# A decode block on one core: `wo` in four loads instead of eight, `w2` in one, the last K ahead of three V, three of the twelve q copies moved to ScalarE, one end barrier less

## The chip, the cores and the metric

One Trainium2 chip, one core used. The metric is the device time of one execution in microseconds (us), median of several runs. The profiler's *span*, from the first to the last recorded instruction of the core, is given for every run too; the rest of the time lies outside it.

## The reference, cut to what matters

```python
B, D, Hq, Dh, W, F = 4, 640, 32, 192, 2048, 1536        # bf16 inputs, one token per batch row
xn = layernorm(x)
q  = xn @ wq                                            # 640 x 6144
p  = softmax(q . k_cache[:, :, -W:, :] * Dh ** -0.5)    # per batch row and head
o  = p . v_cache[:, :, -W:, :]
out = x + o @ wo + (silu(xn @ w1) * (xn @ w3)) @ w2     # wo 6144 x 640, w1 and w3 640 x 1536
```

K and V windows are 32 heads of 3 MB each; with the weights, 223 MB have to come in for very little arithmetic.

## The kernel before

Every head has one K and one V transfer of 3 MB, issued by one queue in program order, K into a ring of two buffers, V into one of three. VectorE (DVE) multiplies K by q, TensorE (PE) adds up the products, a chain over four engines makes the softmax weights `z`, PE multiplies them with V. The projections by `wo` and the feed-forward part run between the heads. Cuts are marked `...`.

The start: `xn`, then q. A K buffer is free for the third head only after the products of the first head, and these need q.

```python
xn = const.tile([B, D], BF16, name="xn")
nc.vector.tensor_scalar_mul(out=xn[:], in0=xc[:], scalar1=rstd[:, 0:1])     # DVE
...
for i, qp in enumerate(qps):                       # 2 x 6 pieces of q, out of PSUM
    dst = qbc[:, (c0 + i) * QC:(c0 + i + 1) * QC]
    if i % 2:
        nc.vector.tensor_copy(out=dst, in_=qp[:])
    else:
        nc.scalar.copy(out=dst, in_=qp[:])
```

The weights `w1`. Its 640 rows do not divide evenly; 64 odd rows lie on a few partitions whose other rows have to be zero, and GpSimd clears them:

```python
we = wopool.tile([LF, 2 * F], BF16, tag="wo", name="w1e")     # LF = 44
nc.gpsimd.memset(we[:], 0.0)                                  # 44 x 3072
nc.gpsimd.memset(wt[0:LF, FH:], 0.0)                          # 44 x 1536
```

The end: the last loads, in this order, and what PE does behind them.

```python
for h in range(H - 2, H):
    add(NU - 6, 0, load_v, h)                # ... K31 is issued between V29 and V30
add(NU - 6, 0, w2_load, 0)                   # w2: columns 0-4, 4-8, 8-11, 11-12 of 12
add(NU - 6, 0, w2_load, 1)
add(NU - 6, 0, wo_load, NG - 2)              # wo: groups of 4 heads, NG = 8
add(NU - 6, 0, wo_load, NG - 1)
add(NU - 6, 0, w2_load, 2)
add(NU - 6, 0, w2_load, 3)
...
nc.scalar.dma_start(out=out..., in_=res[...])
```

## Time and profile before

| | kernel before |
|---|---|
| time, median of 3 runs | 525.95 us (525.63 to 526.19) |
| span of the profiled run | 523.8 us |
| last landing of data | 520.75 us |
| DVE makes `xn` | 11.35 to 13.39 us |
| first product K times q | 32.25 us |
| third K issued | 41.62 us |

How to read it: the transfers fill the whole span (the load queue's packets take 99.2% of the 16 engines' time), so an engine matters only where it delays the *issue* of a transfer or works on after the last landing (at the end). The prediction below shows the profile lines for this and reads them.

### The profile page before, as it was taken

The numbers are of one execution on the slowest core, as the hardware profiler recorded it, in microseconds if no ns is written. First come the engines' busy times: TensorE is split into PE (matmuls) and PEld (weight loads), VectorE is DVE, ScalarE is ACT, GpSimd is POOL, SyncE is SP. The second block draws the span as 40 slices with busy tenths as digits, with TensorE's granted clock in tenths as the row PEclk, the third lists the DMA queues.
The fourth block names the chain that finished last, engine by engine and source line by source line (L and its number), as shares of the span: only waits on it lengthen the run. The fifth ranks groups of instructions, "written<-read, shape, count | busy, mean of one in ns | idle before, by whom it ended". The sixth has DMA issues, their size and how long they took to land.

```text
span 523.8 us, 4820 instructions
## 1 busy us (share of the span) xinstructions
PE 361.8 (69%) x2336; PEld 75.9 (14%) x1643; DVE 340.9 (65%) x413; ACT 55.8 (11%) x176; POOL 5.6 (1%) x12
## 2 busy tenths in 40 slices
PE   0965866887668776667547768586686876675685
PEld 0100111121111111111111111111111111111122
DVE  3268853687656767577646877466667766667671
ACT  2111111111001110101100111001101110011111
POOL 4000000000000000000000000000000000000000
PEclk9979886898878998789997988889878898889988
DMA  9999999999999999999999999999999999999996
GB/s 389 422 443 425 433 431 432 428 433 432 430 435 428 437 418 446 424 437 426 434 434 429 432 434 429 435 427 435 425 437 434 427 437 431 430 434 425 441 418 275
DMA packets 11904, 223.26 MB, mean 426 GB/s; under 512 B 1332, under 2 KB 1608, under 8 KB 3052
## 3 DMA queue, kind: packets, MB, share of 16 engines
q1 hardware_dynamic: 11868, 222.96, 99.2%
q8 instruction: 15, 0.25, 0.2%
q14 instruction: 5, 0.04, 0.0%
q10 hardware_dynamic: 16, 0.01, 0.0%
HBM read 222.96 MB, written 0.01 MB: 426 GB/s over the span
## 4 chain that ended last, share of the span: by engine, by line
DMA 60%; PE 20%; DVE 15%; ACT 3%; issue 1%; SPq 1%
DMA kt<-in_A_k_cache_dram 44%; PE ps L288 11%; DMA w<-in_B_w_dram 11%; DVE pr L277 10%; DMA vt<-in_A_v_cache_dram 5%; PE po L361 4%; PE qps L243 3%; DVE sc L296 2%; ACT ex L324 1%; DVE z L332 1%; DMA x_sb<-in_A_x_dram 1%; PE mt L318 1%; ACT L324 0%; ACT negm L321 0%; PE mt L305 0%
## 5 line engine op out<-in xcount | busy, mean ns | idle before, releaser
L288 PE MATMUL ps<-pr,idb 128*128 128x512 bf16 x768 | 214.7, 422 | 137.6 <-DVE pr L277 137.5
L277 DVE TENSOR_TENSOR pr<-kt,qbc 128x3072 bf16<-128x3072 bf16 x128 | 223.5, 1746 | 104.0 <-DMA kt<-in_A_k_cache_dram 104.0
L296 DVE TENSOR_REDUCE sc<-ps 128x16 f32<-128x512 f32 x128 | 87.1, 681 | 2.7 <-PE ps L288 2.6
L340 PE MATMUL o_ps<-vt,z 128*8 128x384 bf16 x1024 | 60.5, 380 | 0.2 <-DVE z L332 0.2
L361 PE MATMUL po<-o_sb,sel_w 128*32 128x192 f32 x128 | 49.2, 518 | 0.6 <-ACT o_sb L343 0.6
L340 PEld LDWEIGHTS <-z 128*8 128x8 bf16 x1024 | 26.2, 95 | 98.8 <-issue 89.2
L332 DVE TENSOR_TENSOR z<-ex,mask_b 128x256 bf16<-128x256 bf16 x32 | 13.5, 423 | 38.6 <-ACT ex L324 38.6
L343 ACT COPY o_sb<-o_ps 128x384 f32<-128x384 f32 x32 | 15.3, 478 | 196.9 <-PE o_ps L340 196.9
L313 ACT ACTIVATE gneg<-gmax 1x128 f32<-1x128 f32 x32 | 9.8, 308 | 162.8 <-DVE gmax L310 162.8
L305 PEld LDWEIGHTS mt<-idf,lmax 128*1 128x1 f32 x32 | 3.2, 101 | 127.5 <-issue 125.5
L361 PEld LDWEIGHTS po<-o_sb,sel_w 128*32 128x32 f32 x128 | 13.8, 130 | 29.4 <-issue 27.9
L288 PEld LDWEIGHTS <-idb 128*128 128x128 bf16 x124 | 12.0, 97 | 39.3 <-issue 32.8
L318 PEld LDWEIGHTS mt<-ones_ff,gneg 1*128 1x128 f32 x64 | 9.6, 186 | 47.1 <-issue 43.7
L243 PE MATMUL qps<-wt,xnT 128*128 128x512 bf16 x59 | 14.9, 412 | 0.1
L318 PE MATMUL mt<-ones_ff,gneg 1*128 1x1 f32 x64 | 12.3, 259 | 0.7 <-ACT gneg L313 0.7
L321 ACT COPY negm<-mt 128x1 f32<-128x1 f32 x32 | 5.1, 159 | 70.4 <-PE mt L318 70.4
L310 DVE TENSOR_REDUCE gmax<-mt 1x4 f32<-1x128 f32 x32 | 8.8, 274 | 5.8 <-PE mt L305 5.8
L348 PEld LDWEIGHTS po<-rsum,tot_w 128*32 128x32 f32 x64 | 4.4, 108 | 51.5 <-ACT ex L324 35.4
L249 DVE CAST qbc<-qps 128x512 bf16<-128x512 f32 x6 | 3.8, 684 | 11.7 <-PE qps L243 11.7
L324 ACT ACTIVATE ex<-sc,negm 128x64 bf16<-128x64 f32 x32 | 11.1, 348 | 1.0
L305 PE MATMUL mt<-idf,lmax 128*1 128x128 f32 x32 | 10.9, 340 | 0.0
L199 PE MATMUL xnT_ps<-idb,xn 4*128 4x4 bf16 x5 | 0.4, 178 | 13.4 <-DVE xn L194 13.4
(74 smaller groups left out, 84.4 us busy)
## 6 DMA issues: line engine op xcount, KB each, us to landing
kt<-in_A_k_cache_dram SPq DMA_DIRECT2D x32, 3072.0 KB, 19.1
vt<-in_A_v_cache_dram SPq DMA_DIRECT2D x32, 3072.0 KB, 25.5
wo_t<-in_A_wo_dram SPq DMA_DIRECT2D x8, 960.0 KB, 20.7
wt<-in_A_wq_dram SPq DMA_DIRECT2D x2, 3072.0 KB
w<-in_B_w_dram SPq DMA_DIRECT2D x1, 1920.0 KB
wt<-in_A_wq_dram SPq DMA_DIRECT2D x1, 1536.0 KB, 19.5
w<-in_B_w_dram SPq DMA_DIRECT2D x1, 1536.0 KB
w<-in_B_w_dram SPq DMA_DIRECT2D x2, 640.0 KB
```

Source lines behind the costliest of these rows:

```text
L243: nc.tensor.matmul(qp[:], lhsT=xnT[:, kc].rearrange("p a b -> p (a b)"), rhs=wq_rows[kc][:, (c0 + i) * QC:(c0 + i + 1) * QC], start=(kc == ...
L277: nc.vector.tensor_tensor(out=pr[:], in0=kts[h][:, g * JQ:(g + 1) * JQ, :], in1=qbc[:, h * Dh:(h + 1) * Dh].unsqueeze(1).to_broadcast([P, ...
L288: nc.tensor.matmul(ps[:], lhsT=idb[:], rhs=pr[:, :, kk * DD:(kk + 1) * DD], start=(kk == 0), stop=(kk == NK - 1))
L296: nc.vector.tensor_reduce(out=scs[h][:, g * JQ:(g + 1) * JQ], in_=pss.pop(u)[:], axis=AX.X, op=ALU.add)
L305: nc.tensor.transpose(out=mt[0:1, 0:P], in_=chs[h][0][:], identity=idf[:])
L313: nc.scalar.activation(out=gneg[:], in_=gmax[:].unsqueeze(1).to_broadcast([1, PB, B]), func=ACTF.Copy, scale=-SCALE)
L318: nc.tensor.matmul(mt[:, P:P + 1], lhsT=gneg[:].rearrange("o p b -> o (p b)"), rhs=ones_ff[:], start=True, stop=True)
L324: nc.scalar.activation(out=ex[:], in_=scs.pop(h)[:], func=ACTF.Exp, bias=negm[:, 0:1], scale=SCALE, accum_out=rsum[:])
L332: nc.vector.tensor_tensor(out=z[:], in0=ex[:].unsqueeze(2).to_broadcast([P, NJ, B]), in1=mask_b[:].unsqueeze(1).to_broadcast([P, NJ, B]), ...
L340: nc.tensor.matmul(o_ps[c * CT:c * CT + 2 * B, :], lhsT=z[:, 2 * jj:2 * jj + 2, :], rhs=vt[:, 2 * jj:2 * jj + 2, :], start=(jj < 4), stop= ...
L343: nc.scalar.copy(out=o_sb[:], in_=o_ps[:])
L361: nc.tensor.matmul(po[sl, 0:Dh], lhsT=sel_w[:, par].rearrange("p a b -> p (a b)"), rhs=o_sb[:, par * Dh:(par + 1) * Dh].rearrange("p (r i) ...
```

## The change

Its intent: fewer and larger packets (`wo` by eight heads, so four loads of 1.9 MB, the last one in three pieces; `w2` in one; the odd `w1` rows in two transfers instead of four), softmax weights of the last head ready before its V, DVE free of the second half of the q copies (three of its six move to ScalarE), and no second barrier behind the clear of the semaphores. With one `wo` buffer instead of two, the odd rows' tile can be larger, and takes all of them. The diff, cut to its core:

```diff
+def one_end_barrier(nc):
+    ...                      # drops all behind the last clear but one GpSimd drain
-    HG: int = 4,
+    HG: int = 8,
+    FG: int = 4,
-    wopool = ctx.enter_context(tc.tile_pool(name="wo", bufs=2))
+    wopool = ctx.enter_context(tc.tile_pool(name="wo", bufs=1))
 def load_k(h):
-        kt = kpool.tile([P, NJ, Dh], BF16, tag="kt")
+        kt = (kpool if h < H - 1 else vpool).tile(...)      # K31 in the V ring, V31 in the K ring
-            if i % 2:
+            if i % 2 and c0 == 0:
                 nc.vector.tensor_copy(out=dst, in_=qp[:])
 def w1_load():
-        we = wopool.tile([LF, 2 * F], BF16, tag="wo", name="w1e")
+        we = wopool.tile([LF, LS, F], BF16, tag="wo", name="w1e")     # LS = 5
         nc.gpsimd.memset(we[:], 0.0)
-        nc.gpsimd.memset(wt[0:LF, FH:], 0.0)
+    early = {H - 1: (NU - 10, -1)}                          # K31 ahead of V29, V30, V31
-    add(NU - 6, 0, w2_load, 0)                              # and 1, wo, wo, w2 2, w2 3
+    WOC = [0, RPP - 5, RPP - 2, RPP]
+    add(NU - 6, 0, w2_load)
+    for i0, i1 in zip(WOC, WOC[1:]):
+        add(NU - 6, 0, wo_load, NG - 1, i0, i1)
```

More of the change, by code (lines that the diff above doesn't have):

```diff
@@ L47, in first_load_first @@
         head.instructions.insert(j, ins)
+def one_end_barrier(nc):
+    for f in nc.python_module().functions:
+        end = f.blocks[2]
+        i = next(i for i, ins in enumerate(end.instructions) if isinstance(ins, mybir.InstISA))
+        keep = next(j for j in range(i + 1, len(end.instructions)) if end.instructions[j].engine == mybir.EngineType.Pool)
+        assert isinstance(end.instructions[keep], mybir.InstDrain)
+        for j in range(len(end.instructions) - 1, i, -1):
+            ins = end.instructions[j]
+            assert isinstance(ins, (mybir.InstDrain, mybir.InstEventSemaphore)), ins
+            if j != keep:
+                del end.instructions[j]
 @with_exitstack
@@ L87 @@
     CT = 32
+    HB = HG * CT // P
     QW = HG * Dh
     RPP = QW // P
+    RW = Dh // RPP
     NU = H * GQ
@@ L95 @@
     assert JQ * DD == 512 and JQ % 2 == 0 and 2 * Dh <= 512 and 2 * N0 == D and N0 <= 512
-    assert (H * Dh) % QC == 0 and NQ % 6 == 0 and QW % P == 0 and Dh == CT * RPP and P == HG * CT and F == HG * CT * FC
-    assert 2 * H * Dh <= NJ * Dh and KBUFS == 2 and VBUFS == 3
+    assert (H * Dh) % QC == 0 and NQ % 6 == 0 and QW % P == 0 and Dh == RW * RPP and CT == HB * RW and P == FG * CT and F == FG * CT * FC
+    assert 2 * H * Dh <= NJ * Dh and KBUFS == 2 and VBUFS == 3 and HB * (Dh + 1) <= 512 and H // HG > 1
     nc.at_finalize(keep_loaded_weights)
     nc.at_finalize(first_load_first)
+    nc.at_finalize(one_end_barrier)
     ctx.enter_context(tc.manual_schedule())
@@ L123, in load_k @@
     def load_k(h):
-        kt = kpool.tile([P, NJ, Dh], BF16, tag="kt")
+        kt = (kpool if h < H - 1 else vpool).tile([P, NJ, Dh], BF16, tag="kt" if h < H - 1 else "vt", name="kt")
         nc.sync.dma_start(out=kt[:].rearrange("q j d -> q (j d)"),
@@ L127, in load_k, with load_v, wo_load @@
         kts[h] = kt
-    def load_v(h, n=1):
-        vt = vpool.tile([P, NJ, Dh], BF16, tag="vt")
-        for j in range(0, NJ, NJ // n):
-            nc.sync.dma_start(out=vt[:, j:j + NJ // n].rearrange("q j d -> q (j d)"),
-                              in_=v_win[:, h].rearrange("b (p j) d -> p b j d", p=PB)[:, :, j:j + NJ // n].rearrange("p b j d -> p b (j d)"))
-        vts[h] = vt
-    def wo_load(hg):
-        wo_t = wopool.tile([P, RPP * D], BF16, tag="wo")
-        nc.sync.dma_start(out=wo_t[:], in_=A_wo[hg * QW:(hg + 1) * QW, :].rearrange("(p i) n -> p (i n)", i=RPP))
-        wos[hg] = wo_t
+    def load_v(h):
+        vt = (vpool if h < H - 1 else kpool).tile([P, NJ, Dh], BF16, tag="vt" if h < H - 1 else "kt", name="vt")
+        nc.sync.dma_start(out=vt[:].rearrange("q j d -> q (j d)"),
+                          in_=v_win[:, h].rearrange("b (p j) d -> p b (j d)", p=PB))
+        vts[h] = vt
+    def wo_load(hg, i0=0, i1=RPP):
+        if i0 == 0:
+            wos[hg] = wopool.tile([P, RPP * D], BF16, tag="wo", name="wo_t")
+        nc.sync.dma_start(out=wos[hg][:, i0 * D:i1 * D],
+                          in_=A_wo[hg * QW:(hg + 1) * QW, :].rearrange("(p i) n -> p i n", i=RPP)[:, i0:i1, :].rearrange("p i n -> p (i n)"))
     x_sb = const.tile([B, D], BF16, name="x_sb")
@@ L201 @@
     nc.vector.tensor_copy(out=xnT[:], in_=xnT_ps[:].unsqueeze(2).to_broadcast([P, KC, PB, B]))
-    KM, PH, LE, LI = KC - 1, P // 2, 3, 4
-    LP, LF, LB = LE * LI, CT + LE * LI, KM * P + PH
-    assert D - LB == 5 * LP + LI and F % LE == 0
+    KM, LE, LI, LS = KC - 1, 3, 4, 5
+    LP, LF = LE * LI, CT + LE * LI
+    PH = D - KM * P - LP * LS - LI
+    LB = KM * P + PH
+    assert PH == P // 2 and F % LE == 0
     xm = ppool.tile([B, 2, PH, 2], BF16, tag="pr", name="xm")
@@ L212 @@
         nc.vector.tensor_copy(out=xm[:, i, :, i], in_=xn[:, KM * P:LB])
-    xe = ppool.tile([B, 3 + LE, LF], BF16, tag="pr", name="xe")
+    xe = ppool.tile([B, LS + LE, LF], BF16, tag="pr", name="xe")
     nc.gpsimd.memset(xe[:], 0.0)
-    for g in range(2):
-        b0 = LB + g * 2 * LP
-        nc.vector.tensor_copy(out=xe[:, 0:2, g * CT:g * CT + LP].rearrange("b s (e i) -> b s e i", i=LI),
-                              in_=xn[:, b0:b0 + 2 * LP].rearrange("b (i e s) -> b s e i", e=LE, s=2))
-    nc.vector.tensor_copy(out=xe[:, 2, 0:LP].rearrange("b (e i) -> b e i", i=LI),
-                          in_=xn[:, LB + 4 * LP:LB + 5 * LP].rearrange("b (i e) -> b e i", e=LE))
+    nc.vector.tensor_copy(out=xe[:, 0:LS, CT:LF].rearrange("b s (e i) -> b s e i", i=LI),
+                          in_=xn[:, LB:LB + LS * LP].rearrange("b (i e s) -> b s e i", e=LE, s=LS))
     for e in range(LE):
-        nc.vector.tensor_copy(out=xe[:, 3 + e, CT + e * LI:CT + (e + 1) * LI], in_=xn[:, LB + 5 * LP:D])
-    NX = KM + 2
-    xw_ps = ps_t.tile([P, NX + 3 + LE, B], BF16, tag="t", name="xw_ps")
+        nc.vector.tensor_copy(out=xe[:, LS + e, e * LI:(e + 1) * LI], in_=xn[:, LB + LS * LP:D])
+    xw_ps = ps_t.tile([P, KM + 2 + LS + LE, B], BF16, tag="t", name="xw_ps")
     for kc in range(KM):
@@ L228, with weights @@
         nc.tensor.transpose(out=xw_ps[:, KM + i, :], in_=xm[:, i].rearrange("b r h -> b (r h)"), identity=idb[0:B, 0:B])
-    for i in range(3 + LE):
-        nc.tensor.transpose(out=xw_ps[0:LF, NX + i, :], in_=xe[:, i, :], identity=idb[0:B, 0:B])
-    xw = const.tile([P, NX, NREP, B], BF16, name="xw")
-    nc.vector.tensor_copy(out=xw[:], in_=xw_ps[:, 0:NX, :].unsqueeze(2).to_broadcast([P, NX, NREP, B]))
-    xl = const.tile([LF, 3 + LE, NREP, B], BF16, name="xl")
-    nc.vector.tensor_copy(out=xl[:], in_=xw_ps[0:LF, NX:, :].unsqueeze(2).to_broadcast([LF, 3 + LE, NREP, B]))
+    for i in range(LS + LE):
+        nc.tensor.transpose(out=xw_ps[0:LF, KM + 2 + i, :], in_=xe[:, i, :], identity=idb[0:B, 0:B])
+    def weights(name, p, c0, c1):
+        t = const.tile([p, c1 - c0, NREP, B], BF16, name=name)
+        nc.vector.tensor_copy(out=t[:], in_=xw_ps[0:p, c0:c1, :].unsqueeze(2).to_broadcast([p, c1 - c0, NREP, B]))
+        return t
+    xw = weights("xw", P, 0, KM)
+    xh = weights("xh", P, KM, KM + 2)
+    xl = weights("xl", LF, KM + 2, KM + 2 + LS + LE)
     qbc = const.tile([P, H * Dh], BF16, name="qbc")
@@ L268, in acc_add @@
             acc_half(i, lhsT, rhs, last=last)
-    po = ps_po.tile([P, Dh + 1], FP32, name="po")
+    po = ps_po.tile([P, HB * (Dh + 1)], FP32, name="po")
+    po_v = po[:, 0:HB * Dh].rearrange("p (i x r) -> p i x r", x=HB, r=RW)
     def x_add(i):
@@ L346, in ge_tot @@
     def ge_tot(h):
-        sl = slice((h % HG) * CT, (h % HG + 1) * CT)
-        nc.tensor.matmul(po[sl, Dh:Dh + 1], lhsT=tot_w[:].rearrange("p a b -> p (a b)"), rhs=rsums.pop(h)[:],
-                         start=True, stop=True)
+        blk, x = (h % HG) // HB, h % HB
+        nc.tensor.matmul(po[blk * CT:(blk + 1) * CT, HB * Dh + x:HB * Dh + x + 1], lhsT=tot_w[:].rearrange("p a b -> p (a b)"),
+                         rhs=rsums.pop(h)[:], start=True, stop=True)
         chs.pop(h)
     def ge_rec(hg):
-        rt = small.tile([P, 1], FP32, tag="rt", bufs=2, name="rt")
@@ L354, in ge_rec @@
-        nc.vector.reciprocal(out=rt[:], in_=po[:, Dh:Dh + 1])
+        rt = small.tile([P, HB], FP32, tag="rt", bufs=2, name="rt")
+        nc.vector.reciprocal(out=rt[:], in_=po[:, HB * Dh:HB * (Dh + 1)])
         rts[hg] = rt
     def ge_sum(h):
-        sl = slice((h % HG) * CT, (h % HG + 1) * CT)
+        blk, x = (h % HG) // HB, h % HB
         o_sb = o_sbs.pop(h)
         for par in range(2):
-            nc.tensor.matmul(po[sl, 0:Dh], lhsT=sel_w[:, par].rearrange("p a b -> p (a b)"),
+            nc.tensor.matmul(po_v[blk * CT:(blk + 1) * CT, :, x, :], lhsT=sel_w[:, par].rearrange("p a b -> p (a b)"),
@@ L362, in ge_sum @@
                              rhs=o_sb[:, par * Dh:(par + 1) * Dh].rearrange("p (r i) -> p i r", i=RPP), start=(par == 0), stop=(par == 1))
     def ge_turn(hg):
-        og = small.tile([P, RPP, CT], BF16, tag="og", bufs=1, name="og")
-        nc.vector.tensor_scalar_mul(out=og[:].rearrange("p i r -> p (i r)"), in0=po[:, 0:Dh],
-                                    scalar1=rts.pop(hg)[:, 0:1])
+        og = small.tile([P, RPP, HB, RW], BF16, tag="og", bufs=1, name="og")
+        nc.vector.tensor_tensor(out=og[:], in0=po_v, in1=rts.pop(hg)[:].unsqueeze(1).unsqueeze(3).to_broadcast([P, RPP, HB, RW]),
+                                op=ALU.mult)
@@ L368, in ge_turn, with ge_proj @@
         oT = small.tile([P, RPP, CT], BF16, tag="oT", bufs=2, name="oT")
-        nc.vector.transpose(out=oT[:].rearrange("p i r -> p (i r)"), in_=og[:].rearrange("p i r -> p (i r)"))
+        nc.vector.transpose(out=oT[:].rearrange("p i r -> p (i r)"), in_=og[:].rearrange("p i x r -> p (i x r)"))
         oTs[hg] = oT
-    def ge_proj(hg, i0, i1):
+    def ge_proj(hg, i0, i1, last=False):
         oT, wo_t = oTs[hg], wos[hg]
         for i in range(i0, i1):
-            acc_add(oT[:, i, 0:B], wo_t[:, i * D:(i + 1) * D])
@@ L378 @@
-    FW = F // HG
+            acc_add(oT[:, i, 0:B], wo_t[:, i * D:(i + 1) * D], last=last and i == RPP - 1)
+    FW = F // FG
     sT = const.tile([P, FW], FP32, name="sT")
@@ L382 @@
     ffn = {}
-    FM, FH = KM * F, KM * F + F // 2
+    FM = KM * F
     def w1_load():
-        w = B_w1
-        wt = fpool.tile([P, FH + F], BF16, tag="w", name="w1")
-        we = wopool.tile([LF, 2 * F], BF16, tag="wo", name="w1e")
+        wt = fpool.tile([P, FM + F // 2], BF16, tag="w", name="w1")
+        we = wopool.tile([LF, LS, F], BF16, tag="wo", name="w1e")
         nc.gpsimd.memset(we[:], 0.0)
-        nc.gpsimd.memset(wt[0:LF, FH:], 0.0)
-        nc.sync.dma_start(out=wt[:, 0:FM], in_=w[0:KM * P, :].rearrange("(p kc) n -> p (kc n)", kc=KM))
-        nc.sync.dma_start(out=wt[:, FM:FH], in_=w[KM * P:LB, :].rearrange("r (h n) -> (r h) n", h=2))
+        nc.sync.dma_start(out=wt[:, 0:FM], in_=B_w1[0:KM * P, :].rearrange("(p kc) n -> p (kc n)", kc=KM))
+        nc.sync.dma_start(out=wt[:, FM:], in_=B_w1[KM * P:LB, :].rearrange("r (h n) -> (r h) n", h=2))
         ffn["w1"], ffn["w1e"] = wt, we
     def w1_low(n):
-        w, wt, we = B_w1, ffn["w1"], ffn["w1e"]
-        if n < 2:
-            b0 = LB + n * 2 * LP
-            nc.sync.dma_start(out=we[n * CT:n * CT + LP, :],
-                              in_=w[b0:b0 + 2 * LP, :].rearrange("(i e s) n -> e i (s n)", e=LE, s=2))
-        elif n == 2:
-            nc.sync.dma_start(out=wt[0:LP, FH:FH + F], in_=w[LB + 4 * LP:LB + 5 * LP, :].rearrange("(i e) n -> e i n", e=LE))
+        b0, we = LB + LS * LP, ffn["w1e"]
+        if n == 0:
+            nc.sync.dma_start(out=we[CT:LF].rearrange("p s n -> p (s n)"),
+                              in_=B_w1[LB:b0, :].rearrange("(i e s) n -> e i (s n)", e=LE, s=LS))
         else:
-            nc.sync.dma_start(out=wt[CT:LF, FH:FH + F // LE], in_=w[LB + 5 * LP:D, :].rearrange("i (e n) -> e i n", e=LE))
+            nc.sync.dma_start(out=we[0:LP, 0, 0:F // LE], in_=B_w1[b0:D, :].rearrange("i (e n) -> e i n", e=LE))
     def w1_in():
@@ L411, in mm @@
         def mm(w, lhsT, rhs, c0=0, start=False, stop=False):
-            nc.tensor.matmul(ps[w * CT:(w + 1) * CT, c0:c0 + rhs.shape[1]], lhsT=lhsT.rearrange("p a b -> p (a b)"), rhs=rhs,
-                             start=start, stop=stop)
+            nc.tensor.matmul(ps[w * CT:(w + 1) * CT, c0:c0 + rhs.shape[1]], lhsT=lhsT.rearrange("p a b -> p (a b)"), rhs=rhs, start=start, stop=stop)
         def main(kc):
-            for w in range(HG):
+            for w in range(FG):
                 mm(w, xw[:, kc], wt[:, kc * F + w * FW:kc * F + (w + 1) * FW], start=(kc == 0), stop=(kc == KM - 1))
         main(0)
-        for w in range(HG):
+        for w in range(FG):
             c0 = FM + (w % 2) * FW
-            mm(w, xw[:, KM + w // 2], wt[:, c0:c0 + FW])
-        for i in range(2):
-            for w in range(HG):
-                mm(w, xl[:, i], we[:, i * F + w * FW:i * F + (w + 1) * FW])
-        for w in range(HG):
-            mm(w, xl[:, 2], wt[0:LF, FH + w * FW:FH + (w + 1) * FW])
+            mm(w, xh[:, w // 2], wt[:, c0:c0 + FW])
+        for i in range(LS):
+            for w in range(FG):
+                mm(w, xl[:, i], we[:, i, w * FW:(w + 1) * FW])
         FE = F // LE
         for e in range(LE):
-            for w in range(HG):
+            for w in range(FG):
                 c0, c1 = max(e * FE, w * FW), min((e + 1) * FE, (w + 1) * FW)
                 if c0 < c1:
-                    mm(w, xl[:, 3 + e], wt[0:LF, FH + c0 - e * FE:FH + c1 - e * FE], c0 - w * FW)
+                    mm(w, xl[:, LS + e], we[:, 0, c0 - e * FE:c1 - e * FE], c0 - w * FW)
         for kc in range(1, KM):
@@ L444, in w3_in @@
         for kc in range(KC):
-            for w in range(HG):
+            for w in range(FG):
                 nc.tensor.matmul(ffn["ps"][w * CT:(w + 1) * CT, :], lhsT=xnT[:, kc].rearrange("p a b -> p (a b)")[:, 0:CT],
@@ L458, with w2_load, ffn_out @@
     w2_v = B_w2.rearrange("(p c) n -> p c n", c=FC)
-    W2C = [0, FC - 8, FC - 4, FC - 1, FC]
-    def w2_load(i):
-        if i == 0:
-            ffn["w2"] = fpool.tile([P, FC, D], BF16, tag="w", name="w2")
-        c0, c1 = W2C[i:i + 2]
-        nc.sync.dma_start(out=ffn["w2"][:, c0:c1, :].rearrange("p c n -> p (c n)"),
-                          in_=w2_v[:, c0:c1, :].rearrange("p c n -> p (c n)"))
-    def ffn_out(i):
-        for c in range(*W2C[i:i + 2]):
-            acc_add(hT[:, c, 0:B], ffn["w2"][:, c, :], last=(c == FC - 1))
+    def w2_load():
+        wt = fpool.tile([P, FC, D], BF16, tag="w", name="w2")
+        nc.sync.dma_start(out=wt[:].rearrange("p c n -> p (c n)"), in_=w2_v.rearrange("p c n -> p (c n)"))
+        ffn["w2"] = wt
+    def ffn_out():
+        for c in range(FC):
+            acc_add(hT[:, c, 0:B], ffn["w2"][:, c, :])
     sched = defaultdict(list)
@@ L475, in add @@
         sched[slot].append((phase, len(sched[slot]), fn, args))
-    ends = {H - 2: (NU - 1, NU), H - 1: (NU + 3, NU + 4)}
+    ends = {H - 3: (NU - 1, NU), H - 2: (NU + 2, NU + 3), H - 1: (NU + 4, NU + 5)}
+    early = {H - 1: (NU - 10, -1)}
     for h in range(H):
@@ L482 @@
         if h >= KBUFS:
-            add((h - KBUFS + 1) * GQ, 0, load_k, h)
+            add(*early.get(h, ((h - KBUFS + 1) * GQ, 0)), load_k, h)
         if h < H - 2:
@@ L503 @@
     e = ends[H - 1][1] + 1
-    for hg in range(NG - 2):
+    for hg in range(NG - 1):
         a = ((hg + 1) * HG - 1) * GQ + L + 3
-        add(hg * HG * GQ + 8, 0, wo_load, hg)
-        add(a, 6, ge_proj, hg, 0, RPP // 2)
-        add(a + 1, 6, ge_proj, hg, RPP // 2, RPP)
+        add(hg * HG * GQ + 17, 0, wo_load, hg)
+        for n in range(4):
+            add(a + n, 6, ge_proj, hg, n * RPP // 4, (n + 1) * RPP // 4)
     add(3, 0, w1_load)
-    for n in range(4):
-        add(4 + 2 * n, 1, w1_low, n)
+    for n in range(2):
+        add(5 + 3 * n, 1, w1_low, n)
     add(13, 7, w1_in)
@@ L518 @@
     add(17, 6, x_add, 1)
+    WOC = [0, RPP - 5, RPP - 2, RPP]
     for h in range(H - 2, H):
         add(NU - 6, 0, load_v, h)
-    add(NU - 6, 0, w2_load, 0)
-    add(NU - 6, 0, w2_load, 1)
-    add(NU - 6, 0, wo_load, NG - 2)
-    add(NU - 6, 0, wo_load, NG - 1)
-    add(NU - 6, 0, w2_load, 2)
-    add(NU - 6, 0, w2_load, 3)
-    add(e - 1, 8, ffn_out, 0)
-    add(e - 1, 8, ffn_out, 1)
-    add(e - 1, 8, ge_proj, NG - 2, 0, RPP)
-    add(e, 6, ge_proj, NG - 1, 0, RPP)
-    add(e, 7, ffn_out, 2)
-    add(e, 7, ffn_out, 3)
+    add(NU - 6, 0, w2_load)
+    for i0, i1 in zip(WOC, WOC[1:]):
+        add(NU - 6, 0, wo_load, NG - 1, i0, i1)
+        add(e, 6, ge_proj, NG - 1, i0, i1, True)
+    add(e - 1, 8, ffn_out)
     for s in sorted(sched):
```

## The prediction

> **What bounds the kernel now.** I read the whole-kernel page first, then time cut into stretches, then the chain of waits, then the last instructions. On the page, the DMA row of the 40 slices and the queue totals:
> ```profile
> DMA  9999999999999999999999999999999999999996
> GB/s 389 422 443 425 433 431 432 428 433 432 430 435 428 437 418 446 424 437 426 434 434 429 432 434 429 435 427 435 425 437 434 427 437 431 430 434 425 441 418 275
> ...
> q1 hardware_dynamic: 11868, 222.96, 99.2%
> q8 instruction: 15, 0.25, 0.2%
> ```
> Every slice but the last is 90% busy or more, at about 430 GB/s, and the load queue's packets fill 99.2% of what 16 engines have in the 523.8 us span. The table by stretch shows where the missing 0.8% lies (columns: length, PE, PEld, DVE, ACT and POOL busy, clock, DMA share, GB/s):
> ```profile
> 0.00:1.10 1.10, 0.00 (x0) 0.00 (x0) 0.06 (x1) 0.00 (x0) 0.46 (x6) 1.00 0.56 134
> 1.10:40.00 38.90, 21.85 (x92) 2.08 (x28) 18.09 (x39) 6.72 (x11) 5.16 (x7) 0.91 0.99 424
> 40.00:280.00 240.00, 167.72 (x1088) 34.87 (x772) 162.26 (x185) 25.44 (x80) 0.00 (x0) 0.88 1.01 432
> 280.00:510.00 230.00, 164.06 (x1069) 35.10 (x754) 158.16 (x183) 21.87 (x79) 0.00 (x0) 0.90 1.00 431
> 510.00:520.40 10.40, 7.49 (x86) 3.55 (x86) 1.90 (x7) 1.39 (x5) 0.00 (x0) 0.84 0.89 369
> 520.40:523.80 3.40, 0.69 (x8) 0.32 (x7) 0.48 (x1) 0.42 (x1) 0.00 (x0) 0.97 0.01 2
> ```
> From 1.1 to 510 us the transfers never pause, while PE and DVE are busy about 70% of the time. The chain of waits passes through DVE and PE too, but where it does, a transfer is running beside them. The chain ends so (start, length, what):
> ```profile
> 465.17 24.49 DMA vt<-in_A_v_cache_dram
> 489.68 30.66 DMA w<-in_B_w_dram
> 520.38 0.76 PE acc L264 x8
> 521.13 0.47 DVE res L542
> ```
> So the last piece of w2 landed, eight matmuls followed, then the copy, the output and the end. The timeline there says who waited for whom:
> ```profile
> 518.65 0.38 DVE L369 STREAM_TRANSPOSE oT<-og 128x192 bf16<-128x192 bf16 x1
> 519.21 0.98 PE L264 MATMUL acc<-wo_t,oT 128*4 128x320 bf16 x12 [0.47 <-DMA wo_t<-in_A_wo_dram]
> 520.38 0.71 PE L264 MATMUL acc<-w,hT 128*4 128x320 bf16 x8 [0.19 <-DMA w<-in_B_w_dram]
> 521.69 0.27 ACTq L543 DMA_DIRECT2D out_dram<-res  x1
> ```
> PE is ready before the data. The bound is therefore one full stream of 223 MB, plus about 1 us ahead of it and 3.3 us behind it. Only three things can move the time: DMA time per byte, a hole in the stream, or the two ends.
>
> [...] The small w1 copies (12 rows on chip, read as 3 x 4 rows) should then use 3 engines: the trace has 1,324 four-byte semaphore packets in the load queue, which is 82 transfers x 16 + 4 x 3, so it agrees. [...]
>
> **The change, part by part.**
>
> *Transfer sizes.* The trace's records of single packets give a median of 912 ns for 24,576 bytes, 573 for 15,360, 291 for 7,680, 196 for 5,120, 149 for 3,840 and 55 for 1,280. Between the first and the third that is 621 ns for 16,896 bytes, 0.0368 ns a byte, which leaves about 9 ns a packet; a semaphore packet takes 9 ns more. A transfer of 128 rows puts 8 packets and one semaphore packet on each engine.
> - wo before: 8 transfers x (8 x 291 + 9) = 18.70 us per engine. After: three of (8 x 573 + 9), 13.78, and a fourth in pieces of 8,960, 3,840 and 2,560 bytes a row, 8 x (338 + 149 + 103) + 27 = 4.75 (first and last worked out by the slope). Sum 18.53; saved 0.17.
> - w2 before: 8 x (196 + 196 + 149 + 55) + 36 = 4.80. After: 8 x 573 + 9 = 4.59. Saved 0.21.
> - The odd w1 rows: the same bytes on the same three engines, 8 packets each instead of 16: about 0.08 saved there, and only there.
> So the stream ends some **0.38 us** earlier. Bytes do not change.
>
> *Last K ahead of three V.* It changes the order, not the amount. Before, the last head's V landed at 511.43 but its product began at 513.30, as its weights z were only done at 513.24. With the K one V (7.3 us) earlier, z is ready long before, and the product begins when V lands, estimated at 511.1. That gains 2 us, but in front of a PE that then waits for wo, so it only buys slack.
>
> *wo by eight heads.* The closing now has 24 matmuls on w2 and 24 on wo, where the sixth group's 12 used to be out of the way at 518.7. After V at 511.1: product 2.7 us (as 513.30 to 516.01), copy and start of the sums 0.6, four f32 sums to about 516.1 (516.58 to 518.16 before), og over 384 columns 0.6 instead of 0.42, transpose 0.58 (the one of that size in the trace, hT). oT is ready near 517.4. w2, landed at 515.6, takes 24 x 0.068 = 1.6 us on PE, to about 518.0. The wo pieces land at 518.3, 519.5 and 520.4 (back from the end by 1.2 and 0.8). Seven chunks are done by 519.3, three by 520.0. After the final landing come 4 matmuls, not 2: one more pair, **+0.14 us**.
>
> *q copies.* Six of 12 copies were DVE's at 682 ns, ACT's take 592. Three move to ACT; ACT's six end near 32.4 us, but the first product needs only the first half of q. DVE now waits for ACT's fourth copy before it clears a bank; the first product moves from 32.25 to about 31.9. The stream has 3 us of K queued then. Worth 0.
>
> *Second end barrier.* After the semaphore clear (523.41) the Pool drain ends at 523.57 and the barrier's last event at 523.80. Leaving it out takes **0.23 us** off the span. The 2.1 us between span and time I cannot see into; I allow 0.1 for other engines leaving sooner.
>
> Sum: -0.38 + 0.14 - 0.23 - 0.1 = -0.57 us, so **525.4 us**.
>
> **Rivals.**
> - *A hole in the stream.* One wo buffer instead of two, K in the V ring, V in the K ring: if the load queue's issuer stalls for a buffer, transfers run out. Against it: a wo load is issued 7 steps of about 4 us after its buffer's last use; K31 needs V26's buffer, used long before; at the last loads some 17 us of transfers should stand in the queue, and steady K loads take a median 19.1 us from issue to landing, 7.3 of it their own. A hole would cost its length, 1 to 7 us: 527 to 532.
> - *Compute sets the end.* Estimated slack at the first wo piece is 0.3 us on PE and 0.9 on DVE. The other DVE multiply of 128x384 from PSUM (hb) took 1.84 us, not 0.6, though on strided columns. If og did, oT comes at 518.6 and the three pieces still fit within about 0.2 us. If more slips: +0.3 to 1 us, about 526.2.
> - *Reordering pays in full.* If the 2 us between V's landing and its product set the end, the time would fall to about 523.5. Against: PE waits for data at 519.21 and 520.38.
> - *Another engine ends last.* The last transfer's 16 engine-landings spread from 517.53 to 520.75, and nine lie in the last 0.4 us. Instruction fetches (15 of 16,384 bytes, about 0.95 us of delay each to one engine) make the spread. A shift of one onto a late engine eats the whole gain; one away gives at most 0.1.
>
> **Range and chances.** No part reaches 2% (10.5 us). The three runs before span 0.56 us, and a fetch that moves is worth up to 0.95, so 524.6 to 526.1. Within 2%: 0.98; the rest is for a hole, or for what I do not see.
>
> **What will show it.** Right: DMA share 1.00 from 1.1 to 510 us; last landing near 520.4; four or so matmuls on wo after it; the last product starting near 511.1; oT before the first wo piece; span near 523.3; no barrier after the clear. Wrong: a stretch with DMA share under 0.97, PE waiting for oT, at the last piece, or a last landing at 520.7 or later in spite of the smaller packet count.

The -0.1 us in it, for what lies beyond the span, rests on no trace.

## More of the kernel before

```profile
11.35 2.04 DVE L194 TENSOR_SCALAR xn<-xc,rstd 4x640 bf16<-4x640 f32 x1
```

Here 640 elements a partition take DVE 2.04 us, from 11.35 to 13.39 us. The same kind of instruction over the same input size, which makes `xc` a little earlier (8.21 to 8.75 us) while GpSimd is idle, takes 0.54 us.

One view it did not open is DVE and GpSimd between 9 and 17 us. These are the timelines of the two (start, length, engine, line, operation, out<-in, sizes), GpSimd (called POOL) first:

```profile
9.07 2.65 POOL L390 MEMSET w1e<- 44x3072 bf16 x1
11.67 1.37 POOL L391 MEMSET w<- 44x1536 bf16 x1
```

## The result, and the profile after

| | before | after |
|---|---|---|
| time, median (6 runs each) | 525.88 us (525.63 to 526.19) | 526.71 us (525.71 to 527.00) |
| ratio | | 1.0013, 95% interval 1.0001 to 1.0026 |
| span, profiled run | 523.8 us | 524.5 us |
| last landing | 520.75 us | 521.47 us |
| `xn` done | 13.39 us | 16.07 us |
| first product | 32.25 us | 34.60 us |
| third K issued | 41.62 us | 44.12 us |

A ratio is the mean time of one kernel's runs over that of the other's of the same rounds, so not quite the ratio of the medians quoted. The kernel became slower by 0.83 us of median where a gain of 0.57 us was predicted, and it lies 0.6 us above the upper end of the range.

**The end went as predicted, but later.** From the kernel after, the chain of waits (start, length, what):

```profile
484.37 37.10 DMA wo_t<-in_A_wo_dram
...
521.51 0.48 PE acc L284 x4
521.99 0.47 DVE res L547
```

and the timeline of its last us:

```profile
512.31 1.47 PE L361 MATMUL o_ps<-vt,z 128*8 128x384 bf16 x32 [0.36 <-DMA vt<-in_A_v_cache_dram]
515.91 0.56 DVE L387 TENSOR_TENSOR og<-po,rt 128x384 bf16<-128x384 f32 x1 [3.75 <-PE po L382]
516.50 0.58 DVE L390 STREAM_TRANSPOSE oT<-og 128x384 bf16<-128x384 bf16 x1
...
519.59 1.72 PE L284 MATMUL acc<-wo_t,oT 128*4 128x320 bf16 x20 [0.87 <-DMA wo_t<-in_A_wo_dram]
521.51 0.44 PE L284 MATMUL acc<-wo_t,oT 128*4 128x320 bf16 x4 [0.21 <-DMA wo_t<-in_A_wo_dram]
```

The last product now starts when V lands, `oT` is ready 2.5 us before the first `wo` piece, PE waits for data, and four matmuls follow the last landing: the copy `res` starts 0.52 us after it, 0.38 before. This order is the prediction's. Its times are not all so: V landed at 512.27, not near 511.1, and the product took 1.47 us, not 2.7 (before, it ran from 513.30 to 516.01 and the granted clock from 513 to 516 us was 0.56; after, it was 1.00 from 512 to 515). What decides is the last landing, 0.72 us later than before.

**The stream has a hole.** The page's row of slices and its line of the load queue, kernel after:

```profile
GB/s 390 424 446 392 437 428 431 432 433 437 430 430 435 429 435 429 430 436 429 432 434 429 435 429 435 430 431 433 431 434 430 430 435 429 431 437 429 435 423 264
...
q1 hardware_dynamic: 11118, 222.96, 99.1%
```

750 packets fewer, as intended. But the fourth slice, 39 to 52 us, moved 392 GB/s where it had moved 425. The DMA row still reads 9 in that slice: tenths hide a hole of half a microsecond, and so did the table of long stretches (1.00 from 40 to 280 us). Cut finely, the same place reads so, before and then after (stretch, length, busy times of PE, PEld, DVE, ACT and POOL, clock, DMA share, GB/s):

```profile
46.00:47.00 1.00, 0.57 (x3) 0.00 (x0) 1.00 (x3) 0.31 (x1) 0.00 (x0) 1.00 1.01 430
47.00:48.00 1.00, 1.00 (x7) 0.19 (x2) 1.00 (x2) 0.00 (x0) 0.00 (x0) 1.00 1.25 524
```

```profile
46.00:47.00 1.00, 0.59 (x3) 0.00 (x0) 0.96 (x3) 0.00 (x0) 0.00 (x0) 1.00 0.66 240
47.00:48.00 1.00, 0.97 (x6) 0.18 (x2) 1.00 (x2) 0.00 (x0) 0.00 (x0) 1.00 1.09 418
```

(A share over 1.00 comes about where packets that reach into the next stretch are counted whole; neighbouring stretches have to be read together.) All that was queued had landed by 46.6 us, and the third K was issued too late to follow on. The issuing queue's timelines, before and after:

```profile
41.62 0.54 SPq L125 DMA_DIRECT2D kt<-in_A_k_cache_dram  x1
```

```profile
44.12 0.54 SPq L143 DMA_DIRECT2D kt<-in_A_k_cache_dram  x1
```

In both kernels that issue waits for DVE's products of the first head (13.5 us in before, 13.4 in after), and these started 2.35 us later. Followed back (q, then `xnT`, then `xn`), the delay begins in one instruction. GpSimd's and DVE's timelines, kernel after:

```profile
9.24 6.49 POOL L410 MEMSET w1e<- 44x7680 bf16 x1
```

```profile
11.44 4.63 DVE L212 TENSOR_SCALAR xn<-xc,rstd 4x640 bf16<-4x640 f32 x1
```

`xn` takes 4.63 us instead of 2.04, and in both kernels it ends some 0.34 us after GpSimd's clears do (15.73 and 16.07; 13.04 and 13.39). The two old clears covered 3072 and 1536 elements of a partition, the new one covers 7680. At 0.86 ns an element (2.65 us over 3072) that is 6.6 us, which could have been worked out beforehand.

The traces show the order, and no mechanism behind it: GpSimd started 2.2 us before `xn`, and `xn` ended 0.34 us behind it, where the like instruction for `xc`, with GpSimd idle, took 0.54 us. That the clear makes `xn` wait was inference at this point; a1 and b1 test it.

**What the hole makes of the end.** The records of single packets let one ask how late each of the 16 engines is, against a stream without a pause. Before, the last landing's shares were 2.0 to 5.3 us late, mean 4.19; after, 2.4 to 6.2, mean 4.82. The mean rises by 0.6 us, and it had done so at 55 us already (2.30 to 2.92): that is the hole. The latest engine rises by 0.96. This is bookkeeping, since lateness is the landing less the stream: with a stream 0.23 us shorter (packets, see below), 0.96 - 0.23 gives back the 0.72 us of the landing. Of the 0.96 only the mean's 0.6 is traced to the hole.

### The profile page after: what moved, and what is told of

The parts are those of the page before. It is cut to its first block, busy times and chain, and to the rows that moved or that the text cites. A ratio compares the mean times of both kernels' runs of the same rounds, so it can differ in the third digit from the quotient of the medians. Undisturbed runs are those within 1.5% of the kernel's fastest.

```text
span 524.5 us, 4807 instructions
## 1 busy us (share of the span) xinstructions
PE 353.5 (67%) x2347; PEld 75.2 (14%) x1652; DVE 340.5 (65%) x397; ACT 57.3 (11%) x179; POOL 8.2 (2%) x11
## 4 chain that ended last, share of the span: by engine, by line
DMA 60%; DVE 19%; PE 16%; ACT 2%; issue 2%; SPq 0%; DVEq 0%
DMA kt<-in_A_k_cache_dram 52%; DVE pr L298 12%; PE ps L309 9%; DMA wo_t<-in_A_wo_dram 7%; PE po L382 3%; DVE sc L317 3%; PE qps L263 1%; DVE z L353 1%; DMA x_sb<-in_A_x_dram 1%; ACT ex L345 1%; DVE xn L212 1%; PE mt L339 1%; ACT L345 0%; PE f_ps L428 0%; ACT negm L342 0%
## 5 line engine op out<-in xcount | busy, mean ns | idle before, releaser
L309 PE MATMUL ps<-pr,idb 128*128 128x512 bf16 x768 | 210.5, 415 | 146.0 <-DVE pr L298 146.0
L361 PE MATMUL o_ps<-vt,z 128*8 128x384 bf16 x1024 | 54.0, 354 | 1.2 <-DMA vt<-in_A_v_cache_dram 1.2
L361 PEld LDWEIGHTS <-z 128*8 128x8 bf16 x1024 | 24.6, 91 | 98.7 <-issue 88.0
L284 PE MATMUL acc<-wo_t,oT 128*4 128x320 bf16 x96 | 10.0, 318 | 1.1 <-DMA wo_t<-in_A_wo_dram 1.1
```

What stands on the lines that cost most here:

```text
L284: nc.tensor.matmul(acc[i * CT:i * CT + B, :], lhsT=lhsT, rhs=rhs[:, i * N0:(i + 1) * N0], start=first, stop=last)
L309: nc.tensor.matmul(ps[:], lhsT=idb[:], rhs=pr[:, :, kk * DD:(kk + 1) * DD], start=(kk == 0), stop=(kk == NK - 1))
L361: nc.tensor.matmul(o_ps[c * CT:c * CT + 2 * B, :], lhsT=z[:, 2 * jj:2 * jj + 2, :], rhs=vt[:, 2 * jj:2 * jj + 2, :], start=(jj < 4), stop= ...
```

## The experiments

The theory: the long clear delays `xn`, so q, so the third K, so a hole, so everything. Rivals: the transfers' new sizes or order cost time, or luck in where instruction fetches fall on the 16 engines.

Eleven kernels ran, each five times or more, beside the kernel before on the same chip. Time minus span, in the table, is the mean over all runs of a kernel.

| run | time, median (us) | ratio to before (95%) | spans of its runs | time minus span |
|---|---|---|---|---|
| kernel before, all 38 of these rounds | medians 525.66 to 525.83 | | 523.6 to 525.9, median 524.0 | 1.81 |
| after, first six | 526.71 | 1.0013 (1.0001, 1.0026) | 523.8 to 525.1 | 1.97 |
| d1, after again | 527.10 | 1.0017 (1.0004, 1.0031) | 524.4 to 525.3 | 1.99 |
| a1, clear held back | 525.61 | 0.9996 (0.9984, 1.0009) | 523.5 to 523.7 | 2.13 |
| a2, the same again | 525.80 | 0.9998 (0.9986, 1.0011) | 523.5 to 523.6 | 2.17 |
| b1, before with a longer clear | 527.04 | 1.0020 (1.0008, 1.0033) | 524.8 to 525.6 | 1.79 |
| f1, before with clears held back | 525.58 | 0.9996 (0.9983, 1.0008) | 523.7 to 523.9 | 1.79 |
| c1, before with one barrier | 526.09 | 1.0005 (0.9992, 1.0017) | 523.5 to 524.8 | 2.16 |
| g1, a1 with both barriers | 525.76 | 0.9997 (0.9985, 1.0010) | 523.7 to 524.2 | 2.00 |
| g3, g1 with `w2` in four | 526.38 | 1.0010 (0.9994, 1.0026) | 524.0 to 525.1 | 1.94 |
| e2, a1 with the old K order | 526.51 | 1.0011 (0.9997, 1.0024) | 523.6 to 524.6 | 2.14 |
| e1, a1 with odd rows on 12 engines | 528.01 | 1.0040 (1.0028, 1.0053) | 525.7 to 526.1 | 2.08 |
| h1, e1 with rows 7 partitions apart | 526.92 | 1.0018 (1.0005, 1.0032) | 524.8 to 525.1 | 2.08 |

### Does the clear do it? a1, b1, d1, a2

a1 leaves the change as it is, but gives the clear something to wait for: one element of the second half of q. So it runs when `xn` is long done (it starts at 23.27 us, and `xn` ends at 12.08).

```diff
         we = wopool.tile([LF, LS, F], BF16, tag="wo", name="w1e")
+        nc.gpsimd.tensor_copy(out=we[0:1, 0, 0:1], in_=qbc[0:1, 4 * QC:4 * QC + 1])
         nc.gpsimd.memset(we[:], 0.0)
```

> The changed kernel, with GpSimd's clear of w1e held back until the third q copy. Clear theory (the 6.49 us clear keeps DVE's xn waiting, 4.63 us instead of 0.5; everything behind it and so the load of K2 is 2.5 us late and the stream runs dry near 46.5 us): xn takes about 0.55 us and ends near 12.0, K2 is issued near 40 us instead of 44.1, DMA share in 46 to 47 us is 1.0 instead of 0.66, and the time falls by 0.4 to 1.0 us, to 525.6 to 526.2. Rival (instruction fetches falling on an engine that already carries the odd w1 rows set the end): the hole goes, but one engine still ends last by itself and the time stays within 0.3 us of the changed kernel's 526.7.

GpSimd's and DVE's timelines, and the stretch of the hole, in a1:

```profile
23.27 6.50 POOL L411 MEMSET w1e<- 44x7680 bf16 x1
```

```profile
11.54 0.54 DVE L212 TENSOR_SCALAR xn<-xc,rstd 4x640 bf16<-4x640 f32 x1
```

```profile
46.00:47.00 1.00, 0.31 (x3) 0.15 (x2) 0.78 (x1) 0.80 (x2) 0.00 (x0) 1.00 1.20 505
```

The clear is as long as ever, `xn` takes 0.54 us, the third K is issued at 39.57, the hole is gone, the last landing is at 520.63 and the time at 525.61. 

b1 is the opposite: the kernel before, with nothing of the change but a clear of the same total length.

```diff
         nc.gpsimd.memset(wt[0:LF, FH:], 0.0)
+        nc.gpsimd.memset(we[:], 0.0)
```

> The kernel before, with one of its GpSimd clears done twice (2.65 us more), nothing else. Clear theory: xn ends near 16.0 us instead of 13.4, K2 is issued near 44.1 us instead of 41.6, DMA share in 46 to 47 us falls to about 0.66 from 1.01, and the time rises by 0.4 to 0.9 us, to 526.3 to 526.8. Rival: the stream has 5 us in hand, the delay is hidden, and the time stays within 0.2 us of 525.9.

GpSimd's and DVE's timelines in b1, and the stretches of the hole:

```profile
9.02 2.65 POOL L390 MEMSET w1e<- 44x3072 bf16 x1
11.62 1.37 POOL L391 MEMSET w<- 44x1536 bf16 x1
12.94 2.65 POOL L392 MEMSET w1e<- 44x3072 bf16 x1
```

```profile
11.29 4.64 DVE L194 TENSOR_SCALAR xn<-xc,rstd 4x640 bf16<-4x640 f32 x1
```

```profile
46.00:47.00 1.00, 0.89 (x5) 0.00 (x0) 1.00 (x1) 0.00 (x0) 0.00 (x0) 1.00 1.55 387
47.00:48.00 1.00, 0.30 (x2) 0.00 (x0) 1.00 (x2) 0.00 (x0) 0.00 (x0) 1.00 0.11 49
```

The old kernel with the new clear is slow too, 527.04 us, a little more than I expected, since its third K came at 45.4 instead of 44.1 us (q itself was 0.9 us later than in the first run of after, as it was in d1 too, and b1 keeps the old copies, worth 0.4). So the clear alone is enough, and nothing else of the change is needed. It shows one thing more: `xn`, which started at 11.29, did not end between one clear and the next. It ended at 15.93, 0.34 us after the third clear (15.59), as it ended some 0.34 us after the last one in before and after.

d1 repeats the changed kernel in the same rounds, and a2 repeats a1 in others.

> The changed kernel unchanged, once more. Clear theory: hole near 46.5 us again, time 526.3 to 527.0. If the engine that an instruction fetch goes to is fixed by the program, the lags of the 16 engines at the last landing are again 2.4 to 6.2 us with one engine of the odd w1 rows struck near 309 us; if it is drawn anew each run, the pattern differs.

> The changed kernel with its clear held back, unchanged, as the base of the next two and to see how far the first run repeats. Clear theory: xn takes about 0.54 us, third K issued near 39.6, DMA share of 46 to 47 us at 1.0, last landing 520.5 to 520.9, time 525.4 to 525.9, ratio to the kernel before 0.998 to 1.001. If the first result was luck in where instruction fetches fell, the landing goes to 521.2 or later and the time to 526.3 or more although the share stays at 1.0.

d1: `xn` 4.63 us, third K at 44.73, last landing 522.08, 527.10 us, just above what was expected. a2: `xn` 0.54, third K at 40.84 (39.6 was expected), last landing 520.48, 525.80 us. The ten runs with the clear held back have spans of 523.5 to 523.7 us, and the eleven without of 523.8 to 525.1 and 524.4 to 525.3. The clear is worth 1.1 to 1.3 us of span (means 523.54 against 524.60 and 524.86). Luck with fetches alone is ruled out: it does not move with the clear. d1's own question is only half answered: its latest engine was 6.8 us late where it had been 6.2, so the pattern did not repeat, but its hole was larger too.

The packet records show the hole grow with the delay. Between 44 and 55 us the 16 engines lose 0.06 us on average in before, a1, a2 and f1 (third K issued at 39.6 to 41.6 us), 0.7 in after (44.12), 0.9 in d1 (44.73) and 1.5 in b1 (45.41). So the slack ended somewhere between 41.6 and 44.1 us. The 0.7 to 0.9 us are less than the 1.1 to 1.3 of span; the rest lies in how late the last engine is against the mean, and is not traced.

### Does an early start pay by itself? f1

```diff
         we = wopool.tile([LF, 2 * F], BF16, tag="wo", name="w1e")
+        nc.gpsimd.tensor_copy(out=we[0:1, 0:1], in_=qbc[0:1, 4 * QC:4 * QC + 1])
         nc.gpsimd.memset(we[:], 0.0)
```

> The kernel before with its two clears held back until the q copies, as was done in the changed one. Its xn falls from 2.04 to about 0.54 us and everything behind it comes 1.5 us earlier (first product near 30.8, third K issued near 40.1). If only a hole in the stream costs time (the share of 46 to 47 us was 1.01 already), time and last landing stay: 525.5 to 526.1, ratio 0.999 to 1.001. If an early start pays by itself, the time falls by up to 1.5 us, to 524.3.

`xn` falls to 0.54 us, but the first product comes at 31.79 and the third K at 41.31, only 0.3 to 0.5 us earlier, not 1.5. That part of the expectation missed. The likely reason, not shown for f1 itself: with an early `xn` the q matmuls run ahead of the last part of `wq`. In a1 they wait 0.46 us for it, until 21.00; in f1 no wait is recorded, but they take 15.83 us instead of 14.93. The last landing is at 520.65 and the time 525.58, so an earlier start without a hole gains nothing that these runs resolve. The spans of its five runs are closer together than those of the kernel before, 523.7 to 523.9 against 523.6 to 525.9.

### The end barrier: c1 and g1

c1 is the kernel before with `one_end_barrier` of the change and nothing else; g1 is a1 without it.

```diff
+    nc.at_finalize(one_end_barrier)          # c1, in the kernel before
-    nc.at_finalize(one_end_barrier)          # g1, in a1
```

> The kernel before, with the second end barrier left out, nothing else. As predicted: the span ends 0.23 us earlier after the output's landing and the time falls by 0.1 to 0.35 us. Rival [...]: the span shortens, the time does not.

> The changed kernel with its clear held back and with the second end barrier kept. In all runs so far time minus span is 1.7 to 1.9 us for kernels with both barriers and 1.9 to 2.7 us for those with one. If leaving the barrier out only moves time from the span to behind it: the span rises from 523.5-523.7 to 523.7-523.9, time minus span falls to 1.7-1.9, the time is 525.4 to 525.7 with every run below 525.9. If the barrier is worth its 0.23 us as I predicted: the span rises just so, time minus span stays at 1.9 to 2.5, the time is 525.8 to 526.1.

In c1 the profile takes 2.45 us from the start of `res` to the end of the span, against 2.67 in before and in f1: the 0.22 us are there. (The mean spans, 523.96 us against 524.21 for the nine runs of before in the same rounds, agree, but single runs scatter by more.) But its five runs have 2.13 to 2.19 us outside the span, and all 38 runs of before 1.74 to 1.87. The time comes out no better (ratio 1.0005). In the changed kernel the same trade is seen less clearly: with one barrier (a1, a2) 1.88 to 2.49 us lie outside the span, with both (g1) 1.93 to 2.06, and g1's span is 0.3 us longer; the time is the same. g1 fitted neither of its two expectations fully: its time outside the span is lower, but not down to 1.9. What the profile counts as saved comes back, at least for the most part, after its last instruction. What happens there it does not show.

### Did the early K only buy slack? e2

```diff
-    early = {H - 1: (NU - 10, -1)}
+    early = {}
```

> Clear held back, and the last K again only one V ahead of the last two (issue order V, K, V, V instead of K, V, V, V). My step that the early K only buys slack: the last product starts 0.8 us or more behind the landing of the last V, near 513.3; oT is ready near 519 instead of 517.1; the last landing stays where it is (520.6) and the time within 0.2 us of the kernel with the clear held back alone, as the sums on the second and third wo piece still come behind the data. Rival (the order is worth time): PE runs behind the last landing by 0.5 us or more and the time rises by 0.4 us or more.

The last landing stays (520.46), but the chain of waits of e2 ends in compute:

```profile
518.98 0.57 DVE og L387
...
519.58 0.59 DVE oT L390
...
520.21 1.84 PE acc L284 x24
522.05 0.47 DVE res L548
```

All 24 matmuls on `wo` come after `oT` at 520.17, and 20 of them should have been done by then. The profiled run is 0.5 us longer than a2's (its span 1.1), the medians differ by 0.7 us; two of the five runs, with spans of 523.6 and 524.0 us, pay little or nothing. The granted clock was 1.00 there, so a slow PE is not the reason. My step failed here and the rival held: with the old order the closing no longer fits. As the trace reads, the early K is not spare slack, it pays for the larger group; the larger group was not taken back in any run.

### The smaller w2 packets: g3

g3 is g1 with `w2` in four transfers.

```diff
-        nc.sync.dma_start(out=wt[:].rearrange("p c n -> p (c n)"), in_=w2_v.rearrange("p c n -> p (c n)"))
+        for c0, c1 in ((0, 4), (4, 8), (8, 11), (11, 12)):
+            nc.sync.dma_start(out=wt[:, c0:c1].rearrange("p c n -> p (c n)"), in_=w2_v[:, c0:c1].rearrange("p c n -> p (c n)"))
```

> As g1, and w2 in four transfers again (rows of 5,120, 5,120, 3,840 and 1,280 bytes, 24 more packets of data and three more of semaphore on each engine). My prediction's per-packet cost makes that 0.21 us: last landing at 520.75, time 0.2 us above g1. By the spacing of packet starts (about 5 ns a packet, some 0.12 to 0.14 us in all) the landing is near 520.65 and the time 0.1 us above g1. Both are close to what the landing varies by itself (520.48 and 520.63 in two runs of one kernel), so a difference under 0.1 us, or over 0.3, would contradict both.

The landing moved from 520.37 to 520.73, which is more than either reckoning, and by the limit of 0.3 us set beforehand it contradicts both. But three runs of the same stream (a1, a2, g1) land between 520.37 and 520.63, so one landing settles little about packets. `res` starts 0.70 us later than in g1; 0.36 of it is this landing, and 0.34 has another reason. A stretch of the end of g1, then of g3 (the clock stands before the DMA share):

```profile
520.00:521.00 1.00, 0.63 (x8) 0.09 (x3) 0.12 (x1) 0.09 (x1) 0.00 (x0) 1.00 0.00 0
```

```profile
520.00:521.00 1.00, 1.00 (x10) 0.56 (x9) 0.00 (x0) 0.00 (x0) 0.00 (x0) 0.50 0.08 31
```

PE was granted half its clock from about 519.6 us on (0.78 from 519 to 520, then 0.50), and the 24 matmuls on `wo` took 2.71 us, where the same 24 took 1.79 in e2. `res` starts 0.86 us after the landing, not 0.52. d1 and h1 have such a stretch at the end too (0.50 from 518 to 521 us in both), a1, a2, g1 and the first run of after do not (1.00 from 516 us on). It is not what made d1 slow: `res` starts 0.60 us after the landing there, so less than 0.1 us is the clock's. Why it falls there is open.

### Who sets the last landing? e1 and h1

Three engines carry the odd `w1` rows, four packets of 15,360 bytes (2.3 us) each: the packet records of after show three chains of four, 573 ns a packet, from 53.44 to 55.80 us. If they were the last ones, sharing the rows among twelve engines would bring the end forward. That a copy of 12 x 1 rows takes twelve engines was the author's estimate; counted in before are 3 semaphore packets for a copy of 3 x 4 rows and 16 for one of 128 rows.

```diff
-    in_=B_w1[LB:b0, :].rearrange("(i e s) n -> e i (s n)", e=LE, s=LS)     # 3 x 4 rows
+    in_=B_w1[LB:b0, :].rearrange("(p s) n -> p (s n)", s=LS)               # 12 rows, xe likewise
```

> Clear held back, and the 12 odd w1 rows of 15,360 bytes as 12 x 1 instead of 3 x 4 rows, so on 12 engines with one packet each (0.57 us) instead of on three with four (2.3 us). If the three engines with these rows set the end, the last landing comes 0.3 to 0.8 us earlier than in the kernel with the clear held back alone, near 520.0, time about 525.1. If engines struck by two instruction fetches set it (2.1 us of lag at the start and twice 1.5 us make 5.1 to 5.4 in the trace, without any of these rows), most of them now carry 0.57 us more, and the landing is 0 to 0.5 us later: 520.6 to 521.1, time 525.6 to 526.1. In both cases the lag of three engines after 65 us falls from about 4.5 to about 2.2, and that of twelve rises to about 2.7.

Neither came: the time is 528.01 us, and *all* engines are late: at 64 us the least late of the 16 is 3.8 us behind a stream without a pause (2.0 in a2), the mean 4.6 (2.8 in a2). Stretches around these rows, a2 and then e1:

```profile
52.00:54.00 2.00, 1.85 (x10) 0.11 (x8) 0.70 (x2) 0.00 (x0) 0.00 (x0) 0.79 0.94 402
54.00:56.00 2.00, 2.00 (x28) 0.84 (x24) 1.00 (x1) 0.00 (x0) 0.00 (x0) 0.50 0.99 427
```

```profile
52.00:54.00 2.00, 1.81 (x18) 0.30 (x16) 0.74 (x2) 0.00 (x0) 0.00 (x0) 1.00 1.44 392
54.00:56.00 2.00, 1.05 (x28) 0.49 (x18) 0.00 (x0) 0.48 (x1) 0.00 (x0) 1.00 0.60 143
```

The twelve packets took up to 1.44 us instead of 0.57, and the packets of 24,576 bytes that started within the next microsecond 2.05 to 2.57 instead of 0.91. The engines lost 1.8 us on average. In e1 the twelve rows lie side by side, on partitions 32 to 43. That their place on chip makes the packets slow was the author's estimate, shown by no run so far. h1 tests it by putting the rows on partitions 32, 39, ... 109, seven apart:

```diff
-    out=we[CT:LF].rearrange("p s n -> p (s n)")
+    out=we[CT:LF:7].rearrange("p s n -> p (s n)")         # LF = 110
```

> As e1_w1_rows_12_engines, with the 12 odd w1 rows on partitions 32, 39, 46 ... 109 instead of 32 to 43. In e1 [...] the packets of 15,360 bytes took up to 1.44 us instead of 0.57 and the next ones of 24,576 up to 2.57 instead of 0.91, and the whole stream ended 2.2 us later. [...] the packets take 0.57 to 0.7 us and the 2.2 us vanish: last landing 520.0 to 521.0, time 525.2 to 526.2. Rival (twelve engines reading neighbouring rows of w1 in DRAM at once hinder each other, or the issue of 12 packets does): the source is the same, so the long packets and the late end stay, time 527.5 to 528.2. [...] the landing also answers what e1 was to tell: under 520.3, the three engines with four rows each had set the end; 520.4 or more, they had not.

Half of it holds. The twelve packets took 0.57 to 0.75 us, the next ones 1.28 to 1.39, the mean lag of the 16 engines at 64 us is 3.6 us against 4.6 in e1 and 2.8 in a2, the last landing is at 521.69 instead of 522.69 and the time 526.92. So where the rows lie matters (522.69 against 521.69 us), but rows seven partitions apart still leave the engines 0.8 us later than four rows on each of three engines. Why places matter, and what the 0.8 us are, no run here tells. The first question stays open as well, as both attempts disturbed the stream.

## Why the prediction was wrong, step by step

- **The start ("Worth 0").** This is the step that failed. It asked what the q copies do to the first product and had it move from 32.25 to about 31.9; it came at 34.60. The copies did their part: from ScalarE's first copy of q's second half to the first product it took 3.22 us in before and b1, and 2.83 in after and d1, so 0.39 us were gained. But the sum had no term for the clear of the odd rows, because it counted only their transfers ("the same bytes on the same three engines"). That term is +2.5 us on the third K's issue (44.12 against 41.62) and, through the hole, 1.1 to 1.3 us of span. Two of the prediction's own signs of being wrong came with it: a stretch with a DMA share of 0.66, and a last landing later than 520.7.
- **"A hole in the stream" as a rival** was the right kind, looked for in the wrong place; its size ("a hole would cost its length, 1 to 7 us") was too large at the lower end, for the engines lost 0.7 us on average in the changed kernel. It was argued away for the late buffers of the stream's end and middle. The "3 us of K queued" is the slack that mattered: the clear took 2.5 us of it, and the working never asked how much of the 3 us is needed: a load issued at 44.12 left a hole although the queue lasted until 46.6. a1 and b1 show the cause in both directions.
- **Packets, -0.38 us.** The mechanism holds, the term was too large. Packet starts follow each other after 908 ns where the packet is recorded as 912 long: neighbours overlap by some 4 ns, so a packet costs about 5 ns, not 9. Adding up the true spacing gives a stream of 515.25 us instead of 515.48, so -0.23.
- **Four matmuls after the last landing, +0.14 us:** right to the digit (0.52 against 0.38 us).
- **End barrier, -0.23 us, and -0.1 us beyond the span.** The first is in the span (c1: -0.22). The second, an allowance without a trace, has the wrong sign: +0.35 us outside it in c1, 2.16 against 1.81. Together no gain is seen.
- **Last K early.** The wait of 1.9 us between V's landing and its product is gone (512.27 to 512.31). The landings of the closing came 1.1 to 1.3 us later than worked out and kept their distances; the product was 1.2 us shorter, and `oT` was ready at 517.08, near the 517.4 worked out, because the two errors cancel: that is luck. "Only buys slack" was wrong in the changed kernel, as e2 shows.
- **Instruction fetches, "about 0.95 us of delay each".** In the packet records a fetch of 16,384 bytes lasts 934 ns, and the data packet behind it 1,406 instead of 912, so all that follows on that engine comes some 1.41 us late, not 0.95. There are 15 such fetches in the kernel before and 16 in the kernel after. That they "make the spread" is shown in part only: before, the 16 landings of one transfer lie within 0.6 us at 46 us and within 3.2 us at the end, and both fetches and the odd rows come in between. In the profiled run of after, one such fetch, near 309 us, seems to have met an engine that was already among the latest, which would explain the 0.3 us by which the latest engine rose more than the mean. Which engine is which is only inferred from their lags, so this part is argued, not shown.

With the clear held back the change comes to 525.61 and 525.80 us, which is the kernel before's time: the shorter stream, the two more matmuls and the barrier (-0.23 + 0.14 - 0.22 + 0.35 us) cancel to nothing that five runs resolve. No version here beats both kernels by more than the noise; of the versions of the change a1 is the one to keep, 1.5 us ahead of d1 in the same rounds.

## What to carry to other kernels

When a change enlarges a tile, follow every instruction that touches it, the clears too: an engine that is 1% busy can stand in front of another (`xn` took 4.63 us beside the clear and 0.54 without it), and the time of a clear grows with the elements in a partition (1.37, 2.65 and 6.49 us for 1536, 3072 and 7680). A stream that looks full in tenths of 13 us can lose half a microsecond at one point; before calling a start-up delay free, subtract it from the queued transfers and cut that place into stretches of 1 us. And check a saving at the end against the time, not the span.
